# Earlier tiles of a transform, a copy on another engine, and a weight queue served behind the others: one change to a fused spectral and feed-forward kernel on one Trainium2 core

## The chip, the core and the metric

The kernel runs on one core of one Trainium2 chip. A core has five engines, each with its own in-order queue of instructions: TensorE (PE: matrix products into PSUM; PEld is its weight load), VectorE (DVE), ScalarE (ACT), GpSimd (POOL) and SyncE (SP, which here only issues DMAs; ACT and POOL issue some too). Engines wait for each other through semaphores. The metric is the time of one execution on the device in microseconds, lower is better, as the median of several runs.

## What is computed

```python
def _A_ref(x, w_r, w_i):
    X = jnp.fft.rfft2(x, axes=(-2, -1)) * (w_r + 1j * w_i)
    return jnp.fft.irfft2(X, s=(S, D), axes=(-2, -1))

def _B_ref(x, w1, w2):
    h = _silu(jnp.einsum("bsd,df->bsf", x, w1))
    return jnp.einsum("bsf,fd->bsd", h, w2)

xn = _layernorm(x, axis=-1)
return x + _A_ref(xn, w_r, w_i) * _silu(_B_ref(xn, w1, w2))
```

S = 2048 tokens, D = 1024, F = 3584, all float32.

## The kernel before, in words

Matmuls run in float16 on numbers split into a high and a low half, three passes for one product. The 2048 tokens are four chunks c of 512.

**The work that fills TensorE.** The first product (xn by w1, `mm1`, PSUM tile `pa`, 24 matmuls of 512 columns, L466 is the matmul) runs over chunks and feature tiles. The second product (h by w2, `mm2`, PSUM tile `pb`, L549 to L551) is made of seven block products m by eight token tiles j by two halves k of 21 matmuls each; `w2_block` and `SUMMED = (4, 5)` say which blocks of w2 enter product m. Its left operand `ht` is loaded by `load_h` from a queue of ScalarE (L525), two token tiles ahead.

**The background work.** Everything else is written as generators that yield between steps, and their matmuls are slipped between the blocks of the two products. The list `bg` holds the layer norm, the transform over d of each chunk (`fd_gen`), the transform over s (matmuls `fx`), and the inverse of each chunk (`i_gen`, in the order `IORDER = (1, 3, 0, 2)`). The list `wq` holds the splitting of w1 and then of w2 (`w2_gen`), and `xq` the scans for maxima.

**fd_gen.** For a chunk: four tiles p of 24 small matmuls into a PSUM tile `fa` (`fa_mat`, L803 to L805; PSUM tag "ft" with two buffers), two ScalarE instructions that empty it into `L0` (`fa_evac`, L812 and L813; two buffers), a butterfly on VectorE per tile, then four stages j of a radix step on VectorE, whose results ScalarE and VectorE split (`high_r`, L884 and L886; `low_r`) and SP stores.

**w2_gen.** One step loads a tile `jr` of w2 four steps ahead (SP, L420), for m = 4 and 5 lets GpSimd add a second block onto a tile three steps ahead (an accumulating DMA, L424), makes the high half on ScalarE (`high`, L257) and the low half of the tile before on VectorE (`low`, L260).

**i_gen.** `load_i` puts four DMAs of `zt`, one of `kk`, and for the first chunk the constants `cis`, on SP. `edge_in` copies the edge frequencies into `zt` (128 partitions by 16 elements). Then `iu` matmuls (L1281 and L1289; four tiles), with a copy `uc` on ScalarE (L1295) and two VectorE instructions `ub` (L1297, L1298) that free the PSUM tile, further VectorE steps, a split `us`, and a second set of matmuls `id`.

**What sets the order.** `work()` is called once after each block of `mm1` and twice for each (m, j) of `mm2`. It hands out one step of `wq`, one of `xq` in seven calls of eight, and then up to three steps of `bg`, as long as the planner's clock for VectorE is not over that for TensorE by more than `LEAD`; a step's yield says what it costs VectorE. The order in which the steps are handed out is the order of their instructions on every engine's queue.

Of the kernel before, what the change touches and what calls it, by code (L numbers as in the profile page):

```python
# [26 lines left out]
IORDER = (1, 3, 0, 2)  # L27
# [105 lines left out]
def spectral_ffn(ctx, tc, x, w_r, w_i, w1, w2, ca, kc, ci, tw, pm, out):  # L133
    nc = tc.nc
# [35 lines left out]
    zps = cp.tile([128, 2, 4, 4, 2], F16, name="zps")  # L170
# [45 lines left out]
    clock = {"pe": 0.0, "dve": 0.0}  # L216
# [16 lines left out]
    def radix4(sign, b, d, o):  # L233

        sub = nc.vector.tensor_tensor
        plus, minus = ((2, 7), (6, 3)) if sign < 0 else ((6, 3), (2, 7))

        def pick(i):
            st = i[1] - i[0]
            stop = i[1] + (1 if st > 0 else -1)  # L240
            return o[:, i[0]:stop:st]

        sw = d[:, 1, ::-1]
        sub(o[:, 0:2], b[:, 0], b[:, 1], op=OP.add)
        sub(o[:, 4:6], b[:, 0], b[:, 1], op=OP.subtract)
        sub(pick(plus), d[:, 0], sw, op=OP.add)
        sub(pick(minus), d[:, 0], sw, op=OP.subtract)
# [207 lines left out]
    done2, ready2, chunks = [0], [-1], [0]  # L455
# [343 lines left out]
    def fa_mat(c, p):  # L799
        ps = pt.tile([128, 8, 128], F32, name=f"fa{c}_{p}", tag="ft")  # L800
        sl, xt = slice(p * 128, (p + 1) * 128), xnT[c]
        for d in range(8):
            nc.tensor.matmul(ps[:, d], xt[:, 0, d, sl], A["ca"][:, 0, d], start=True, stop=False)  # L803
            nc.tensor.matmul(ps[:, d], xt[:, 0, d, sl], A["ca"][:, 1, d], start=False, stop=False)
            nc.tensor.matmul(ps[:, d], xt[:, 1, d, sl], A["ca"][:, 0, d], start=False, stop=True)  # L805
        psa[c, p] = ps

    def fa_evac(c, p):
        ps = psa.pop((c, p))
        t0 = A["p"].tile([128, 8, 2, 65], F32, name=f"L0_{c}_{p}", tag="L0", bufs=2)  # L810
        nc.gpsimd.memset(t0[:, :, 1, 0:1], 0.0)
        nc.scalar.activation(t0[:, :, 0], ps[:, :, 0:65], AF.Copy)  # L812
        nc.scalar.activation(t0[:, :, 1, 1:64], ps[:, :, 65:128], AF.Copy)  # L813
        l0[c, p] = t0

    def fd_gen(c):
# [51 lines left out]
            tt(v[:, 1, 0:1], ee[:, 0, 0, 0:1], ee[:, 1, 0, 0:1], op=OP.subtract)  # L868

        for i in range(6):  # L870
            if i < 4 and c:
                fa_mat(c, i)
            if 1 <= i <= 4 and (c or i > 2):
                fa_evac(c, i - 1)
            yield 0
            if i >= 2:
                yield from bfly(i - 2)
            yield 0
        o, sp, total, both = {}, {}, {}, {}

        def high_r(j):
            room = ap.tile([128, 2048 + 256 * len(THREE)], F16, name=f"Rs{c}_{j}", tag="Rs", bufs=2)
            both[j] = room[:, 2048:].rearrange("p (q h k) -> p q h k", h=2, k=128)
            nc.scalar.activation(both[j][:, :, 0], total[j], AF.Copy, scale=2.0**-21)  # L884
            sp[j] = room[:, 0:2048].rearrange("p (q h k) -> p q h k", h=2, k=256)
            nc.scalar.activation(sp[j][:, :, 0], o[j], AF.Copy, scale=2.0**-21)  # L886

        def low_r(j):
            nc.vector.scalar_tensor_tensor(sp[j][:, :, 1], o[j], 2.0**-21, sp[j][:, :, 0], op0=OP.mult, op1=OP.subtract)
            nc.vector.scalar_tensor_tensor(both[j][:, :, 1], total[j], 2.0**-21, both[j][:, :, 0], op0=OP.mult, op1=OP.subtract)  # L890
            defer(2, lambda: nc.sync.dma_start(vd[j][:, :, c], sp[j]))
            defer(2, lambda: nc.sync.dma_start(vs[j][:, :, c], both[j]))

        for j in range(4):
            sl = slice(128 * j, 128 * j + 128)
            if j:
                high_r(j - 1)
            b = ap.tile([128, 2, 2, 128], F32, name=f"Rb{c}_{j}", tag="Rb", bufs=1)
            d = ap.tile([128, 2, 2, 128], F32, name=f"Rd{c}_{j}", tag="Rd", bufs=1)
            nc.vector.tensor_tensor(b, vt[:, 0:2, :, sl], vt[:, 2:4, :, sl], op=OP.add)  # L900
            nc.vector.tensor_tensor(d, vt[:, 0:2, :, sl], vt[:, 2:4, :, sl], op=OP.subtract)
            if j:
                low_r(j - 1)
            r = ap.tile([128, 8, 128], F32, name=f"Ro{c}_{j}", tag="Ro", bufs=1)
            radix4(-1, b, d, r)
            o[j] = r.rearrange("a (q r) k -> a q (r k)", r=2)
            total[j] = ap.tile([128, len(THREE), 128], F32, name=f"vt{c}_{j}", tag="E", bufs=1)
            some = o[j][:, THREE[0]:THREE[-1] + 1]
            nc.vector.tensor_tensor(total[j], some[:, :, 0:128], some[:, :, 128:256], op=OP.add)
            clock["dve"] -= 0.8  # L910
            yield 3.9
        high_r(3)
        yield 0.5
# [332 lines left out]
    def edge_in(c):  # L1246
        zt = C["z"][c]
        if c % 2:
            zt = zt.rearrange("m (e q h l i) -> m e q h l i", e=2, q=4, h=2, l=8)
            nc.gpsimd.tensor_copy(zt[:, :, :, :, 0, 0], zps[:, :, c])  # L1250
        else:
            zt = zt.rearrange("m (q h r l i) -> m q h r l i", q=4, h=2, r=2, l=8)
            nc.gpsimd.tensor_copy(zt[:, :, :, :, 0, 0], zp[:, c].rearrange("m r q h -> m q h r"))

    def i_gen(c):
        ip = C["p"]
        tt, stt = nc.vector.tensor_tensor, nc.vector.scalar_tensor_tensor
        if c == IORDER[0]:
            edge_in(c)
# [187 lines left out]
        for p in range(5):  # L1447
            if p < 4:
                mat2(p)
            if p:  # L1450
                bfly(p - 1)
            if p == 3 and c != IORDER[-1]:
                edge_in(IORDER[IORDER.index(c) + 1])
            yield 3.4 if p else 0.3
# [13 lines left out]
    def slot(q):  # L1468
        while q:
            job = q[0]  # L1470
            cost = job.step()
            if not job.done:
                return cost
            if q and q[0] is job:
                q.pop(0)
        return 0
# [19 lines left out]
    with tc.manual_schedule():  # L1496
        bg, wq, xq = [], [], []
# [20 lines left out]
        def after(ev):  # L1518
            settle()
            fresh_ev[0] = ev  # L1520
            tick()
            work()

        def work():
            slot(wq)
            count[0] += 1
            if count[0] % 8:
                slot(xq)
            clock["dve"] = max(clock["dve"], clock["pe"] - 1.0)
            for _ in range(3):  # L1530
                if clock["dve"] > clock["pe"] + LEAD or hold[0] or slot(bg) == PAUSE:
                    break

        nc.gpsimd.memset(ones, 1.0)
        idle = ones.bitcast(F16)
# [34 lines left out]
        for c in range(4):  # L1570
            add(bg, fd_gen(c))
# [69 lines left out]
        for n, (m, j) in enumerate(seq):  # L1641
# [14 lines left out]
            for k in range(2):  # L1656
                while ready2[0] < m * NP + 7 * k + 6:
                    slot(wq)
                mm2(m, j, ps, k)
                if k == 0:  # L1660
                    settle()
                    load_parts(m, j)
                    ahead_rows(m, j)
                    if (m, j) == (6, 6):
                        load_parts(m, 7)
                        ahead_rows(m, 7)
                    tick()
                    work()
# [43 lines left out]
```

## Time and profile before

| | us |
|---|---|
| three runs | 1228.38, 1229.09, 1229.40 |
| median | 1229.09 |
| profiled execution, its own time | 1229.27 |
| its span (first to last instruction) | 1227.5 |
| TensorE busy | 1211.4 |
| VectorE busy | 1003.7 |
| ScalarE busy | 496.1 |
| GpSimd busy | 140.2 |

All times in the views are microseconds from the start of the span. A row of the timeline gives start, duration, engine, line, operation, out<-in, partitions by elements, the count, and in brackets how long the engine had stood idle before it and what released it. In the chain of waits a row gives start, duration and what the chain passed through. Names in the profile are without the buffer numbers that the order of instructions shows.

### The profile page before, as it was taken

To read this page: it belongs to the slowest core of one execution; us is meant where nothing else is said; L and a number is where in the kernel's file an instruction comes from. 1 tells how busy PE (TensorE), PEld (TensorE's weight loads), DVE (VectorE), ACT (ScalarE), POOL (GpSimd) and SP (SyncE) were. 2 spreads that over 40 slices of the span, in tenths; PEclk is the share of its full clock that TensorE was granted. 3 is DMA by queue.
4 is the path that set the end of the run, shared out by engine and by line. 5 is a ranking of instruction groups with operands and counts; after the bars stand their busy time and mean duration, and the time that the engine had idled before them with its cause. 6 is when DMAs were issued, how large, how long until landed. Compare 5 with 4: busy or idle time off the path is not lost.

```text
span 1227.5 us, 19143 instructions
## 1 busy us (share of the span) xinstructions
PE 1211.4 (99%) x6992; PEld 615.1 (50%) x6992; DVE 1003.7 (82%) x2006; ACT 496.1 (40%) x670; POOL 140.2 (11%) x256
## 2 busy tenths in 40 slices
PE   8999999999999999999999999999999999999998
PEld 5544445445444544445445555554445554455545
DVE  7778997898798798958969989995377876997766
ACT  6775553455375654434423222221122322333212
POOL 3320100002010000201101121152111111000000
PEclk9999999999999999999999999999999999999999
DMA  8887585747678978489998999977979999996677
GB/s 251 184 195 188 165 255 180 211 130 214 192 254 276 317 231 270 146 259 208 188 282 279 263 253 233 315 255 221 269 218 302 264 338 310 305 364 244 224 249 274
DMA packets 285055, 299.98 MB, mean 244 GB/s; under 512 B 48928, under 2 KB 211744, under 8 KB 284576
## 3 DMA queue, kind: packets, MB, share of 16 engines
q1 hardware_dynamic: 264944, 239.95, 66.9%
q10 hardware_dynamic: 15840, 50.67, 11.8%
q0 software_dynamic: 4176, 8.13, 3.6%
q8 instruction: 55, 0.90, 0.3%
q14 instruction: 40, 0.33, 0.1%
HBM read 188.05 MB, written 104.35 MB: 238 GB/s over the span
## 4 chain that ended last, share of the span: by engine, by line
PE 59%; DMA 15%; DVE 14%; ACT 3%; issue 3%; SPq 1%; POOL 1%; ACTq 0%; DVEq 0%; POOLq 0%
PE pa L466 33%; PE pb L551 7%; PE pb L549 7%; PE pb L550 7%; DMA jr<-in_B_w_dram 2%; PE id L1371 2%; DMA jr<-ws 1%; DVE Z L1124 1%; DVE w L260 1%; DMA cis<-in_ci_dram 1%; DMA ht<-hd_dif 1%; ACT xp L750 1%; DMA vq<-vd 1%; DMA zd<-zq 1%; DMA zt<-zd 1%
## 5 line engine op out<-in xcount | busy, mean ns | idle before, releaser
L466 PE MATMUL pa<-xnT,w 128*128 128x512 f16 x2688 | 584.3, 379 | 1.3 <-ACT w L257 0.7
L466 PEld LDWEIGHTS <-w 128*128 128x128 f16 x2688 | 261.2, 98 | 312.7 <-issue 1.2
L549 PE MATMUL pb<-w,ht 128*128 128x512 f16 (+2 forms) x812 | 300.4, 372 | 0.0
L550 PE MATMUL pb<-w,ht 128*128 128x512 f16 (+2 forms) x812 | 300.4, 372 | 0.0
L551 PE MATMUL pb<-w,ht 128*128 128x512 f16 (+2 forms) x812 | 300.3, 372 | 0.0
L551 PEld LDWEIGHTS <-ht 128*128 128x128 f16 x812 | 79.4, 98 | 91.1
L549 PEld LDWEIGHTS <-ht 128*128 128x128 f16 x812 | 79.5, 98 | 86.7
L550 PEld LDWEIGHTS <-ht 128*128 128x128 f16 x812 | 79.4, 98 | 86.8
L475 ACT ACTIVATE h<-pa,s 128x512 f32<-128x512 f32 x112 | 75.6, 677 | 77.6 <-PE pa L466 60.2
L257 ACT ACTIVATE w<-jr,sc 128x512 f16<-128x512 f32 x98 | 68.4, 713 | 86.4 <-DMA jr<-in_B_w_dram 45.6
L260 DVE SCALAR_TENSOR_TENSOR w<-jr,sc,w 128x512 f16<-128x512 f32 x98 | 71.3, 743 | 18.8 <-ACT w L257 18.8
L257 ACT ACTIVATE hosum<-hr,hs 128x1536 f16<-128x1536 f32 x28 | 44.0, 1573 | 87.5 <-DVE hr L505 34.9
L260 DVE SCALAR_TENSOR_TENSOR hoone<-h,hs,hoone 128x2048 f16<-128x2048 f32 x28 | 65.6, 2342 | 7.2 <-ACT hoone L257 7.2
L257 ACT ACTIVATE hoone<-h,hs 128x2048 f16<-128x2048 f32 x28 | 55.9, 1995 | 28.6 <-issue 11.1
L504 DVE TENSOR_TENSOR hr<-h 128x1024 f32<-128x1024 f32 x28 | 34.1, 1219 | 21.8 <-ACT h L475 21.8
L260 DVE SCALAR_TENSOR_TENSOR hosum<-hr,hs,hosum 128x1536 f16<-128x1536 f32 x28 | 50.7, 1810 | 1.4 <-ACT hosum L257 1.4
L257 ACT ACTIVATE w<-w1r,rs 128x1024 f16<-128x1024 f32 x28 | 31.9, 1143 | 37.7 <-DVE w L260 24.2
L642 ACT ACTIVATE pl<-pl,c 128x512 f32<-128x512 f32 (+2 forms) x28 | 17.7, 656 | 70.2 <-DVE pl L618 43.6
L424 POOL DMA_DIRECT2D jr<-in_B_w_dram x28 | 24.6, 999 | 180.3 <-DMA jr<-in_B_w_dram 89.7
L1124 POOL TENSOR_TENSOR Z<-yb 128x32 f32<-128x32 f32 x32 | 16.2, 525 | 209.0 <-DVE yb L1103 202.2
L1033 ACT ACTIVATE zq<-Z,zs 128x1024 f16<-128x1024 f32 x16 | 18.4, 1148 | 52.5 <-DVE Z L1124 25.6
L260 DVE SCALAR_TENSOR_TENSOR w<-w1r,rs,w 128x1024 f16<-128x1024 f32 x28 | 35.6, 1273 | 2.3 <-ACT w L257 2.2
(239 smaller groups left out, 1571.6 us busy)
## 6 DMA issues: line engine op xcount, KB each, us to landing
w1r<-in_B_w_dram SPq DMA_DIRECT2D x28, 512.0 KB, 6.6
hd_sum<-hosum SPq DMA_DIRECT2D x56, 256.0 KB, 2.9
hd_one<-hoone SPq DMA_DIRECT2D x56, 256.0 KB, 4.0
hd_dif<-hoone SPq DMA_DIRECT2D x56, 256.0 KB, 4.3
w2m<-in_B_w_dram SPq DMA_DIRECT2D x28, 512.0 KB, 5.6
ht<-hd_dif ACTq DMA_DIRECT2D x32, 448.0 KB, 9.2
jr<-in_B_w_dram SPq DMA_DIRECT2D x56, 256.0 KB, 6.7
ht<-hd_sum ACTq DMA_DIRECT2D x32, 448.0 KB, 5.7
```

What stands on the lines that cost most here:

```text
L257: nc.scalar.activation(hi, raw, AF.Copy, scale=scale)
L260: nc.vector.scalar_tensor_tensor(lo, raw, scale, hi, op0=OP.mult, op1=OP.subtract)
L424: nc.gpsimd.dma_start(raw[n], w2_block(*todo[n], 1), accum_op=OP.add)
L466: nc.tensor.matmul(ps, w[:, wh, d], xt[:, xh, d], start=(n == 0), stop=(n == 23))
L475: nc.scalar.activation(hq[:, 2 * (c % 2) + f % 2], ps, AF.Silu, scale=s1[:, f:f + 1])
L504: tt(sums[:, 0:2], hq[:, 0::2], hq[:, 1::2], op=OP.subtract)
L549: nc.tensor.matmul(ps, hh[:, 0], w[:, 0], start=first, stop=False)
L550: nc.tensor.matmul(ps, hh[:, 0], w[:, 1], start=False, stop=False)
L551: nc.tensor.matmul(ps, hh[:, 1], w[:, 0], start=False, stop=last)
L1033: nc.scalar.activation(zqs[q][:, 0, :, 16 * j:16 * j + 16], zs_[u], AF.Copy, scale=zs)
L1124: eng.tensor_tensor(Z[:, ns, pos], x0[:, :, ls], x1[:, :, ls], op=o_)
L1371: nc.tensor.matmul(ps[:, g, cols], us[g][:, uh, 4 * r + p], C["ci"][:, ch, g, r, cols], start=(r == 0 and n == 0), stop=(r == 1 and n == 2 ...
```

## The change

Five edits. (1) In `fd_gen` the chunks after the first no longer issue one tile per step: tile 2's matmuls come at step 0 and tile 3's at step 3, and the emptying of tiles 1, 2, 3 at steps 0, 3 and 4. (2) Tiles 0 and 1 of the next chunk are issued in stages j = 2 and 3 of the chunk before, with the emptying of tile 0 at j = 3. (3) The planner's clock for VectorE gets 0.5 back per stage in place of 0.8. (4) `edge_in` for the first inverse chunk (c = 1) copies on VectorE in place of GpSimd. (5) In the second product (`chunks[0] == 4`) the step of `wq` is handed out behind those of `bg` in a call of `work()`, in place of ahead of them.

```diff
@@ fd_gen
         for i in range(6):
-            if i < 4 and c:
-                fa_mat(c, i)
-            if 1 <= i <= 4 and (c or i > 2):
-                fa_evac(c, i - 1)
+            if i in (0, 3) and c:
+                fa_mat(c, 2 + i // 3)
+            if i in (0, 3, 4) and (c or i):
+                fa_evac(c, max(i, 2) - 1)
             yield 0
...
         for j in range(4):
+            if j > 1 and c < 3:
+                fa_mat(c + 1, j - 2)
+                if j > 2:
+                    fa_evac(c + 1, 0)
             sl = slice(128 * j, 128 * j + 128)
...
-            clock["dve"] -= 0.8
+            clock["dve"] -= 0.5
             yield 3.9
@@ edge_in
-            nc.gpsimd.tensor_copy(zt[:, :, :, :, 0, 0], zps[:, :, c])
+            (nc.vector if c == IORDER[0] else nc.gpsimd).tensor_copy(zt[:, :, :, :, 0, 0], zps[:, :, c])
@@ work
-            slot(wq)
+            if chunks[0] < 4:
+                slot(wq)
             count[0] += 1
             if count[0] % 8:
                 slot(xq)
...
+            if chunks[0] == 4:
+                slot(wq)
```

Three places show how instructions move. The first is ScalarE around chunk 3's transform over d (`fa_p` is the PSUM tile of tile p, `L_3_p` what it is emptied into, `h` the evacuation of the first product's `pa`, `w` and `junk` work on the weights). Before:

```order
L257 ACTIVATE w_21_4185<-w1r_3823,rs_228 128x1024
L390 ACTIVATE junk,w2m<-w2m_3977 128x1024
L812 ACTIVATE L_3_0_4219<-fa_0_4126 128x8x65
L813 ACTIVATE L_3_0_4219<-fa_0_4126 128x8x63
L475 ACTIVATE h_8_1_4109<-pa_16_4151,s_229 128x512
L390 ACTIVATE junk,w2m<-w2m_4016 128x1024
L812 ACTIVATE L_3_1_4292<-fa_1_4194 128x8x65
L813 ACTIVATE L_3_1_4292<-fa_1_4194 128x8x63
```

Of the change:

```order
L812 ACTIVATE L_3_0_4032<-fa_0_3927 128x8x65
L813 ACTIVATE L_3_0_4032<-fa_0_3927 128x8x63
L884 ACTIVATE Rs_2_4036<-vt_2_3966 128x2x128
L886 ACTIVATE Rs_2_4036<-Ro_2_3961 128x4x256
L475 ACTIVATE h_8_0_3916<-pa_16_3968,s_229 128x512
L390 ACTIVATE junk,w2m<-w2m_3883 128x1024
L884 ACTIVATE Rs_3_4093<-vt_3_4050 128x2x128
L886 ACTIVATE Rs_3_4093<-Ro_3_4045 128x4x256
L475 ACTIVATE h_8_0_3916<-pa_17_4052,s_229 128x512
L812 ACTIVATE L_3_1_4168<-fa_1_4007 128x8x65
L813 ACTIVATE L_3_1_4168<-fa_1_4007 128x8x63
```

Tile 0 of chunk 3 is now emptied ahead of the last two splits (`Rs`) of chunk 2, and tile 1 three evacuations of `pa` after it. On TensorE two blocks of `pa` lie between `fa_0` and `fa_2` of that chunk before, and now three beside `fa_1`.

The second place is VectorE and ScalarE at the first inverse chunk (`w_3_1` is half of w2's tiles for m = 3, `jr` a loaded tile of it, `kept` an evacuation of `pb`, `ub` the inverse's first VectorE step). VectorE before, where the copy of zt's edge stood on GpSimd behind the joins of jr_8644, jr_8675 and jr_8701 as `L1250 COPY zt_8581<-zps 128x16`:

```order
L260 SCALAR_TENSOR_TENSOR w_3_1_8544<-jr_8504,sc_234,w_3_1_8544 128x512
L260 SCALAR_TENSOR_TENSOR w_3_1_8544<-jr_8542,sc_234,w_3_1_8544 128x512
L598 TENSOR_TENSOR kept_7103<-kept_7103,pb_5_8652 128x512
L260 SCALAR_TENSOR_TENSOR w_3_1_8544<-jr_8572,sc_234,w_3_1_8544 128x512
L260 SCALAR_TENSOR_TENSOR w_3_1_8544<-jr_8619,sc_234,w_3_1_8544 128x512
L598 TENSOR_TENSOR kept_7180<-kept_7180,pb_6_8710 128x512
L1297 TENSOR_TENSOR ub_0_8840<-iu_0_8788,uc_0_8838 128x512
```

VectorE with the change:

```order
L260 SCALAR_TENSOR_TENSOR w_3_1_8544<-jr_8542,sc_234,w_3_1_8544 128x512
L598 TENSOR_TENSOR kept_7103<-kept_7103,pb_5_8652 128x512
L260 SCALAR_TENSOR_TENSOR w_3_1_8544<-jr_8588,sc_234,w_3_1_8544 128x512
L1254 COPY zt_8577<-zps 128x16
L260 SCALAR_TENSOR_TENSOR w_3_1_8544<-jr_8619,sc_234,w_3_1_8544 128x512
L598 TENSOR_TENSOR kept_7180<-kept_7180,pb_6_8710 128x512
L1301 TENSOR_TENSOR ub_0_8840<-iu_0_8788,uc_0_8838 128x512
```

On SP the load of jr_8572 stood ahead of the four zt loads, kk and cis; that of jr_8588, which takes its place in the sequence of w2's tiles, now stands behind them, next to jr_8619. On ScalarE the two issues of ht_0 stand, before and now, between the high half of that tile (jr_8572, now jr_8588) and that of jr_8619.

The third place is ScalarE at the third inverse chunk (`w_5_1`: w2's tiles for m = 5; `pl` a sum of partial products). Before:

```order
L525 DMA ht_7_1_10428<-hd_one_1_97 128x1792
L257 ACTIVATE w_5_1_10302<-jr_10299,sc_234 128x512
L1295 ACTIVATE uc_0_10520<-iu_0_10470 128x512
L1341 ACTIVATE up_0_10526<-ub_0_10522 128x8
L1342 ACTIVATE up_0_10526<-ub_0_10522 128x8
L642 ACTIVATE pl_4_1_10383<-pl_4_1_10383,c_233 128x512
```

Of the change:

```order
L525 DMA ht_7_1_10428<-hd_one_1_97 128x1792
L1299 ACTIVATE uc_0_10516<-iu_0_10466 128x512
L1345 ACTIVATE up_0_10522<-ub_0_10518 128x8
L1346 ACTIVATE up_0_10522<-ub_0_10518 128x8
L257 ACTIVATE w_5_1_10302<-jr_10299,sc_234 128x512
L642 ACTIVATE pl_4_1_10383<-pl_4_1_10383,c_233 128x512
```

The high half of jr_10299 moved from ahead of the inverse's three instructions to behind them.

## The prediction

> **What bounds the kernel now.** I read the page first: share of busy time, granted clock, DMA.
>
> ```profile
> span 1227.5 us, 19143 instructions
> PE 1211.4 (99%) x6992; PEld 615.1 (50%) x6992; DVE 1003.7 (82%) x2006; ACT 496.1 (40%) x670; POOL 140.2 (11%) x256
> PEclk9999999999999999999999999999999999999999
> ```
>
> TensorE is busy 99% of the span at full granted clock. The changed program holds the same matmuls as the old one, only some in another place. So time can leave only where TensorE stands still, and the next view is what it waited for (engine, line, what it waited for: us in total, times, longest).
>
> ```profile
> PE tp L759 <- ACT x L750: 2.7, 2, 2.5
> PE iu L1281 <- POOL zt L1250: 2.6, 1, 2.6
> PE iu L1289 <- DVE ub L1298: 1.8, 1, 1.8
> PE fa L803 <- ACT L L813: 1.3, 1, 1.3
> ```
>
> The row for tp belongs to the start, which the change leaves alone. The other three are single events, one wait each. The timeline places them and gives their full size (start, duration; a matmul's 0.38 overlaps its successor, which starts 0.22 later).
>
> ```profile
> 410.27 2.97 PE L466 MATMUL pa<-xnT,w 128*128 128x512 f16 x13
> 414.58 0.22 PE L803 MATMUL fa<-cas,xnT 128*128 128x128 f16 x1 [1.34 <-ACT L L813]
> 876.51 0.38 PE L550 MATMUL pb<-w,ht 128*128 128x512 f16 x1
> 876.73 0.38 PE L551 MATMUL pb<-w,ht 128*128 128x512 f16 x1
> 879.72 2.85 PE L1281 MATMUL iu<-kk,zt 128*128 128x128 f16 x48 [2.61 <-POOL zt L1250]
> 1036.64 0.38 PE L551 MATMUL pb<-w,ht 128*128 128x512 f16 x1
> 1038.83 1.55 PE L1289 MATMUL iu<-kk,zt 128*128 128x129 f16 x24 [1.81 <-DVE ub L1298]
> ```
>
> Start to start, less the 0.22 that a matmul takes anyway (876.73 − 876.51): 879.72 − 876.73 − 0.22 = 2.77 us lost at the first inverse chunk's iu_0; 1038.83 − 1036.64 − 0.22 = 1.97 at the third inverse chunk's iu_2; and, since the thirteen pa matmuls end at 413.24 and the last of them began 0.38 earlier, at 412.86, 414.58 − 412.86 − 0.22 = 1.50 at chunk 3's fa_2. Together 6.24 us, 0.51% of the span. That is the most that these edits can win.
>
> **First edit: the transform's first tiles sooner (the fd_gen loops and the planner's 0.5).** The chain of waits before 414.58 runs on ScalarE:
>
> ```profile
> 413.95 0.59 ACT L L813
> 414.58 0.22 PE fa L803
> 401.32 0.22 PE L805 MATMUL fa<-cas,xnT 128*128 128x128 f16 x1
> ```
>
> fa_2 needs the PSUM buffer of fa_0, whose last matmul starts at 401.32; ScalarE, in its order, empties it only by 413.95 + 0.59 = 414.54, 13.2 us later. Before, two products of 24 matmuls lie between fa_0 and fa_2, 2 × 24 × 0.216 = 10.4 us (0.216 is the 0.22 unrounded: thirteen starts from 410.27 to 412.86 are twelve steps). After the change, three lie there (15.6 us), beside fa_1, so a ScalarE exactly as late as now is 2.4 us early. The evacuations themselves are the same two instructions per tile, moved and not added. fa_3 behind fa_1 has at least five products of cover. The work that is brought forward, two tiles of 24 small matmuls, costs nothing: it is issued while VectorE runs the previous chunk's radix stages. Without that cover it would cost its own wait on ScalarE, 1.34, as now. Term: −1.50; bounds −1.50 and 0.
>
> **Second edit: the copy of zt's edge from GpSimd to VectorE, first inverse chunk only.** The chain of waits up to 879.72, and the engines' timelines beside it:
>
> ```profile
> 849.21 11.20 DMA zt<-zd
> 860.43 14.25 DMA cis<-in_ci_dram
> 874.75 2.60 DMA jr<-in_B_w_dram
> 877.35 0.61 POOL jr L424 x2
> 878.41 1.27 POOL zt L1250
> 876.66 2.74 POOL L424 DMA_DIRECT2D jr<-in_B_w_dram  x3 [41.31 <-DMA jr<-in_B_w_dram]
> 875.37 0.72 ACT L257 ACTIVATE w<-jr,sc 128x512 f16<-128x512 f32 x1 [21.93 <-DMA jr<-in_B_w_dram]
> 876.12 0.75 DVE L260 SCALAR_TENSOR_TENSOR w<-jr,sc,w 128x512 f16<-128x512 f32 x1 [11.22 <-ACT w L257]
> 401.78 0.15 DVE L299 TENSOR_TENSOR ep<-e 128x1 f32<-128x1 f32 x1
> ```
>
> zt itself does not make iu_0 late: GpSimd takes its queue in order, and three joins (L424, accumulating loads of w2) stand ahead of the copy, waiting for jr loads that the SP queue put behind zt and cis. On VectorE the three joins are no longer ahead. But something else is, as the order shows: the low half L260 of jr_8588, whose load the third edit has just moved behind zt, kk and cis on the SP queue. Its place there is the one that jr_8619 has before, whose high half starts at 875.37. So the new path is high 0.72, low 0.75, then the copy: 875.37 + 0.75 + 0.75 = 876.87 (the old rows' own starts, 876.12 then 0.75), and the copy's 16 elements a lane. No row shows that copy on VectorE: 0.15 by the nearest small VectorE row, 1.27 by GpSimd's own. I take 0.15, since it is VectorE that runs it: zt complete at 877.0, with 878.1 as the other end. TensorE is there at 876.95, or at 875.45 if the 1.50 of the first edit arrives in full. So iu_0 waits between nothing and 877.05 − 875.45 = 1.6 us, against 2.77 + 1.50 that could be won up to here. Two things shorten that: loads issued from planner steps move up with TensorE, and the two ht_0 loads of the next product, which now run inside the same stretch, leave it (next edit). I take 0.5 as the rest: term −2.77 + 0.5 = −2.27; bounds −2.77 and −0.1 (copy 1.27, no transfer earlier).
>
> [...]
>
> **Third edit: w2's step behind those of transform and inverse in the second product.** It changes no count, only who stands first on ScalarE, VectorE, GpSimd and the SP queue when one call of the planner issues several. The gain is in the chain to 1038.83:
>
> ```profile
> 1036.25 0.72 ACT L257 ACTIVATE w<-jr,sc 128x512 f16<-128x512 f32 x1 [11.88 <-DMA jr<-in_B_w_dram]
> 1036.87 0.59 ACT uc L1295
> 1037.48 0.69 DVE L1297 TENSOR_TENSOR ub<-iu,uc 128x512 f32<-128x512 f32 x1 [7.99 <-ACT uc L1295]
> 1038.18 0.61 DVE ub L1298
> ```
>
> ScalarE stands 11.88 us at the high half of jr_10299, until its accumulating join has landed, and only behind it comes the copy uc that iu_2 waits for through ub. In the new order uc stands ahead of that high half and the inverse step on VectorE ahead of the low half. ScalarE was free for 11.88 us, so uc runs as soon as iu_0 is done: iu_2 does not wait. Term −1.97; bounds −1.97 and 0 (the next high half takes the place). VectorE stood still for 7.99 us before ub; the ub step now falls in there, which also eases the us chain behind it.
>
> What it costs: high halves of 0.72 now stand ahead of some ht issues on ScalarE's queue. In the second product's m = 1 that is one more ahead of ht_2:
>
> ```profile
> 729.88 3.18 ACTq L525 DMA_DIRECT2D ht<-hd_dif  x2
> DMA to landing us min/median/max: 9.4/10.8/13.8
> 742.41 0.38 PE L549 MATMUL pb<-w,ht 128*128 128x512 f16 x1
> ```
>
> Issued at 729.88, landed 9.4 later at the earliest, 739.3; pb_2 starts at 742.41 without a wait, so its margin is 0 to 3.1, and the delay 0.7 to 1.4: a cost of 0 to 1.4, where I take 0.2. The one large move is at the first inverse chunk: ht_0's two issues stand behind the high half of jr_8588, so they go from 854.48 to about 875.4.
>
> ```profile
> 854.48 4.86 ACTq L525 DMA_DIRECT2D ht<-hd_sum  x2
> 875.45 0.81 ACTq L525 DMA_DIRECT2D ht<-hd_sum  x2
> 882.41 0.38 PE L549 MATMUL pb<-w,ht 128*128 128x512 f16 x1
> ht<-hd_sum ACTq DMA_DIRECT2D x32, 448.0 KB, 5.7
> ```
>
> They are used by the next product's pb_0, which follows the half block of 21 matmuls at 882.41 (21 × 0.216 = 4.5) and iu_2 (1.3): 888.3 before, about 884.5 with the gains (1.50 + 2.27 earlier). Issue 875.45 + 5.7 (the median of this form) = 881.2, with 13.8 from the slowest ht seen 889.3: cost 0 to 4.9, taken as 0.1.
>
> Sum: −1.50 − 2.27 − 1.97 + 0.2 + 0.1 = −5.44. Against the profiled execution's own 1229.27 (1.8 outside its span) that is 1223.83; the median of the runs is 0.18 lower, so 1223.65, rounded 1223.7.
>
> **The rivals.** What a measurement here can tell from no change is about 0.2%, 2.46 us: faster is below 1226.6, slower above 1231.6.
>
> A. *The copy stays late.* VectorE's copy ends at 878 or after (a slow copy, a hold by GpSimd, or jr_8588 landing later than jr_8619 did) and TensorE still starts iu_0 near 879.7. Then the first edit's gain is lost in the same wait too, since TensorE merely arrives earlier, and only the third term and what lies behind 880 is won: −1.97 + 0.3, 1227.4; with a copy ending at 878.1 it is −1.6 more, 1225.8. For it: the copy's place directly behind a w2 low half. Against: the 2.6 us between 877.05 and 879.67.
>
> B. *Transfers take the gain back.* The DMA shares are high where the gains fall (columns: window, sum, five engines, clock, DMA share, GB/s):
>
> ```profile
> 880.00:960.00 80.00, 80.00 (x546) 43.77 (x543) 58.18 (x154) 22.29 (x41) 13.28 (x17) 1.00 0.96 260
> 960.00:1040.00 80.00, 78.19 (x517) 42.06 (x516) 62.33 (x151) 22.26 (x42) 7.69 (x11) 1.00 0.96 304
> 1040.00:1140.00 100.00, 100.00 (x626) 52.42 (x624) 89.35 (x190) 34.33 (x64) 1.13 (x2) 1.00 0.85 297
> ```
>
> If loads cannot move up with TensorE, later ht or w2 tiles become the wait: half of 5.44 gone is 1226.4, all but the third term 1227.1. Against: TensorE does not wait once for an ht or a w2 tile in the second product now, through 260 us of such shares.
>
> C. *Slower: ht_0 starves pb_0.* One mechanism: w2's step behind the inverse's puts jr_8588's load behind zt, kk and cis, its high half waits for it on ScalarE (21.93 now for jr_8619), and ht_0 queues behind that. If ht_0 comes with ht_1 and the three joins in one burst, it may land far after 884.5. From 884.5 + 5.4 = 889.9 on (14.5 us after issue) nothing is left of the gain; from 892.4 on, 17 after issue, the kernel is slower. A landing at 896 gives 1235. Longest seen: 13.8, so a small chance.
>
> D. *The transform's edit does not do what it says.* ScalarE's lateness grows by as much as the tiles move, and fa_2 waits as now: 1.50 back, 1225.2. It counts as faster still.
>
> **How the numbers follow.** Forecast as summed, 1222.4 to 1225, 0.62; D 0.06; A 0.13, of which a third ends below 1226.6; B 0.12, half of it below; C 0.07 (0.06 slower, 0.01 within). Faster: 0.62 + 0.06 + 0.05 + 0.06 = 0.79. Same: 0.08 + 0.06 + 0.01 = 0.15. Slower 0.06. The low end is all three stalls gone with no cost, 1229.09 − 6.24 = 1222.85, less 1.0 for what an easier VectorE may give elsewhere and the spread of the runs: 1221.8. The high end takes in A and B to 1228.3. The likeliest case's own range is 1222.4 to 1225.0.
>
> **What would show it.** In the new profile's list of TensorE's waits the row fa <- ACT L should be gone; the row iu <- POOL zt replaced by none or by iu <- DVE zt of under 1.6; the row iu <- DVE ub gone. TensorE's busy time should stay near 1211 and the span fall to about 1222. New rows pb <- DMA ht near 742, 805 or 885 would show the third edit's cost. A row iu <- DVE zt above 2 means A; pb <- DMA ht of more than 5 means C; many small rows pb <- DMA mean B. The prediction fails if the order of issue moves a transfer that I have taken as fixed.

## The result, and the profile after

The change is slower. Ten runs of each kernel, side by side: 1234.61 us (1229.64 to 1238.35) against 1229.59 us (1225.93 to 1232.63) before, ratio 1.0039 with a 95% interval of 1.0025 to 1.0053. The profiled execution took 1233.81 us. Its page:

```profile
span 1232.0 us, 19135 instructions
PE 1216.2 (99%) x6992; PEld 617.0 (50%) x6992; DVE 1003.4 (81%) x2007; ACT 494.4 (40%) x670; POOL 126.8 (10%) x255
PEclk9999999999999899999999999999999999999999
```

The span grew by 4.5 us and TensorE's busy time by 4.8, with the same matmuls. One slice of the granted clock shows an 8. What TensorE waited for:

```profile
PE pa L466 <- ACT h L475: 4.5, 2, 4.3
PE eps L1165 <- POOL edge L1158: 2.0, 1, 2.0
PE tp L759 <- ACT x L750: 1.8, 3, 1.2
```

All three waits that the change was to remove are gone: no row for fa, none for iu. Two others stand in their place, one in the first product and one at the edge matmuls (`eps`) of the transform over s. TensorE and VectorE at the first and third inverse chunk:

```profile
886.23 2.84 PE L1285 MATMUL iu<-kk,zt 128*128 128x128 f16 x48
1036.07 2.91 PE L1293 MATMUL iu<-kk,zt 128*128 128x129 f16 x48
1043.35 1.54 PE L1293 MATMUL iu<-kk,zt 128*128 128x129 f16 x24
881.86 0.75 DVE L260 SCALAR_TENSOR_TENSOR w<-jr,sc,w 128x512 f16<-128x512 f32 x1 [8.34 <-ACT w L257]
882.53 0.20 DVE L1254 COPY zt<-zps 128x16 f16<-128x16 f16 x1
```

The copy ran behind the low half of w2, as the order said, took 0.20 us, and was done 3.5 us before iu_0. The iu rows carry no brackets: nothing was waited for. For iu_0 that is partly luck: TensorE came to it at 886.23, where it came at 876.95 before, because the two new waits had held it up. In the run with three repairs (below), where they are gone, iu_0 does wait, 0.71 us start to start.

The first new wait, on TensorE, ScalarE and the SP queue (SPq rows are the DMAs that SP issues):

```profile
398.47 5.34 PE L466 MATMUL pa<-xnT,w 128*128 128x512 f16 x24
408.07 12.21 PE L466 MATMUL pa<-xnT,w 128*128 128x512 f16 x45 [4.26 <-ACT h L475]
406.08 0.42 ACT L884 ACTIVATE Rs<-vt 128x256 f16<-128x256 f32 x1 [8.74 <-DMA vs<-Rs]
407.35 0.67 ACT L475 ACTIVATE h<-pa,s 128x512 f32<-128x512 f32 x1
396.12 1.20 SPq L498 DMA_DIRECT2D hd_sum<-hosum  x2
398.88 0.91 SPq L891 DMA_DIRECT2D vd<-Rs  x1
399.85 1.04 SPq L892 DMA_DIRECT2D vs<-Rs  x1
```

ScalarE stood 8.74 us before the split `Rs` of stage 3. There are two Rs buffers, so stage 3 takes over that of stage 1, whose stores SP issued only at 398.88 and 399.85; the second landed at 406. The planner defers these stores by two ticks (a tick comes with each call of the planner), and on SP's queue they stood behind the stores of `hosum` (L498, a part of h), for which SP had waited 5.9 us. The same splits of stages 1 and 3 before, with the store between them:

```profile
384.45 0.40 ACT L884 ACTIVATE Rs<-vt 128x256 f16<-128x256 f32 x1
394.43 0.71 SPq L892 DMA_DIRECT2D vs<-Rs  x1
405.41 0.40 ACT L884 ACTIVATE Rs<-vt 128x256 f16<-128x256 f32 x1
```

There the split of stage 3 came 11 us after the store was issued and waited for nothing. In the change, behind the split in ScalarE's queue stood the evacuation of pa (L475, 407.35), without which TensorE had no PSUM buffer. The last matmul before began at 398.47 + 5.34 − 0.38 = 403.43, so 408.07 − 403.43 − 0.22 = 4.42 us were lost.

The granted clock behind it, and behind the second new wait (window, sum, busy time of five engines, clock, DMA share, GB/s):

```profile
408.00:410.00 2.00, 1.93 (x5) 0.71 (x5) 2.00 (x3) 1.00 (x3) 0.00 (x0) 0.50 1.03 174
412.00:414.00 2.00, 2.00 (x9) 0.80 (x8) 1.86 (x5) 2.00 (x4) 0.85 (x2) 0.79 1.08 391
414.00:416.00 2.00, 2.00 (x11) 0.87 (x9) 1.97 (x6) 2.00 (x3) 0.00 (x0) 1.00 1.06 344
816.00:820.00 4.00, 4.00 (x13) 1.55 (x12) 4.00 (x8) 0.00 (x0) 0.00 (x0) 0.62 1.03 403
```

After the stall TensorE ran at half its clock until 412.84, 4.8 us from its start at 408.07: its matmuls start 0.43 us apart there, 5 of them in the 2 us from 408, where 11 do at full clock from 414, 0.22 apart. Adding up how much later than 0.216 us each start came gives 2.37 us behind the first stall and 1.71 behind eps, whose wait is here:

```profile
812.21 0.40 PE L1165 MATMUL eps<-edge,perm 128*128 128x24 f32 x2 [2.01 <-POOL edge L1158]
811.79 0.37 POOL L1158 COPY edge<-xsv 128x24 f32<-128x24 f32 x1
810.00 1.02 POOL L1128 TENSOR_TENSOR Z<-yb 128x32 f32<-128x32 f32 x2 [16.77 <-DVE yb L1107]
```

GpSimd's edge copies stand behind its share of the Z step and came 2.18 us late (start to start). The balance: −6.24 for the three stalls, +4.42 + 2.37 at 408, +2.18 + 1.71 at eps: +4.44, against a span 4.5 longer. What remains is small: TensorE was 0.4 us ahead by 130 us, and eps' 18 matmuls took 0.2 us longer (2.34 against 2.11).

### The profile page after: what moved, and what is told of

Its sections match the earlier page's. It is cut to its first block, busy times and chain, and to the rows that moved or that the text cites. A ratio compares the mean times of both kernels' runs of the same rounds, so it can differ in the third digit from the quotient of the medians.

```text
span 1232.0 us, 19135 instructions
## 1 busy us (share of the span) xinstructions
PE 1216.2 (99%) x6992; PEld 617.0 (50%) x6992; DVE 1003.4 (81%) x2007; ACT 494.4 (40%) x670; POOL 126.8 (10%) x255
## 4 chain that ended last, share of the span: by engine, by line
PE 71%; DMA 9%; DVE 9%; ACT 3%; issue 2%; SPq 1%; ACTq 0%; POOL 0%; DVEq 0%
PE pa L466 33%; PE pb L551 11%; PE pb L549 11%; PE pb L550 11%; PE id L1375 2%; DMA jr<-ws 2%; DMA ws<-wd 2%; DMA ht<-hd_dif 1%; ACT xp L750 1%; DMA wq<-in_A_w_r_dram 1%; PE iu L1293 1%; PE iu L1285 1%; DMA wq<-in_A_w_i_dram 1%; DMA ht<-hd_sum_d 1%; DVE Z L1128 1%
## 5 line engine op out<-in xcount | busy, mean ns | idle before, releaser
L475 ACT ACTIVATE h<-pa,s 128x512 f32<-128x512 f32 x112 | 75.2, 676 | 62.8 <-PE pa L466 47.7
```

Source lines behind the costliest of these rows:

```text
L475: nc.scalar.activation(hq[:, 2 * (c % 2) + f % 2], ps, AF.Silu, scale=s1[:, f:f + 1])
```

## The experiments

Unless said otherwise, each was timed side by side with the kernel before; the ratio is to it. Theory S: the splits of the transform over d now stand too near each other for their buffer's store.

**Which edit loses.** Four kernels: edits 1 to 3 alone, edit 5 alone, edit 4 alone, edits 4 and 5. They differ from the kernel before only by those lines of the diff above.

> Edits 1 to 3 alone (transform over d, planner's 0.5). Theory S (the split of stage 3 now stands two blocks of pa behind that of stage 1, whose buffer it reuses, and waits on ScalarE for that buffer's store; TensorE then starves for an evacuation and its clock falls): the stall of 4.4 us near 408 is here again with the same granted clock of 0.5 behind it, the wait on fa (1.5) is gone, so 4.4 + 2.2 - 1.5 = 5.1 us slower than before, ratio 1.003 to 1.006. Rival W (the w2 queue behind the others is what loses): 1.5 us faster, ratio 0.9988.

> Edit 5 alone (w2's step behind those of transform and inverse in the second product). Theory S: the wait of iu on ub (1.97) goes, the wait of iu on GpSimd's copy stays about as it is (2.8), so 1 to 2 us faster if the edge matmuls (eps), which had 0.3 us to spare before, are in time; if they are late by 2 us with a clock drop, up to 3 us slower. Rival W: 4 us slower or more, with eps waiting on GpSimd and the granted clock down behind it, and nothing wrong near 408.

> Edit 4 alone (the first inverse chunk's edge copy on VectorE). Both theories: the wait of iu on GpSimd's copy (2.77) goes, since with w2's step ahead as before no load of w2 behind cis stands ahead of the copy on VectorE but that of jr_8572, which is early; 2 to 2.8 us faster, ratio 0.9978 to 0.9984; 0 if the copy is held until GpSimd's joins are through.

> Edits 4 and 5 without the transform's. Theory S: both waits of iu gone, 4 to 4.7 us faster (ratio 0.9962 to 0.9968), less up to 3 if eps is late here too; granted clock 1.0 throughout the first product. Rival W: not faster, since the loss comes with edit 5.

| edits | median us | ratio | 95% interval |
|---|---|---|---|
| 1 to 3 | 1236.55 | 1.0050 | 1.0034 to 1.0067 |
| 5 | 1228.39 | 0.9987 | 0.9972 to 1.0001 |
| 4 | 1227.52 | 0.9979 | 0.9966 to 0.9992 |
| 4 and 5 | 1228.01 | 0.9987 | 0.9973 to 1.0002 |

TensorE's waits with edits 1 to 3 alone:

```profile
PE pa L466 <- ACT h L475: 5.8, 2, 4.2
PE iu L1285 <- POOL zt L1254: 1.8, 1, 1.8
PE iu L1293 <- DVE ub L1302: 1.6, 1, 1.6
PE s L266 <- ACT h L475: 1.1, 1, 1.1
```

The loss is in edits 1 to 3, as expected: the stall near 408 is back, with another near 532 (1.29 + 1.80 us start to start), and the two waits of iu are still there because nothing was done about them. Rival W falls. Edit 4 alone, too, gave what was expected of it (0.9978 to 0.9984).

Edit 5 alone left neither wait of iu in its profile, though the one on GpSimd had been expected to stay. It went by a narrow margin: the three joins still stand ahead of the copy on GpSimd, but the first is issued at 873.93 in place of 876.66, the copy ends at 876.93, and iu_0 starts at 876.99. The same order makes iu_0 wait 1.67 us for that copy in the run with early edge copies (below). So edits 4 and 5 overlap in part; that together they gained no more than each, within these intervals, has a second reason in eps, which in the profile of both was late by 0.88 and then lost 1.5 us of clock. The expectation of 4 to 4.7 us for both holds only with its clause on eps. With edit 4 alone, the copy and GpSimd's joins ran at the same time:

```profile
877.18 4.51 POOL L424 DMA_DIRECT2D jr<-in_B_w_dram  x5 [41.09 <-DMA jr<-in_B_w_dram]
877.33 0.20 DVE L1250 COPY zt<-zps 128x16 f16<-128x16 f16 x1
```

0.20 us, as in the changed kernel: the hold by GpSimd that rival A and the expectation name did not show.

**Does the store make the stall?** The stores of the splits one planner tick sooner, all else as in the change.

```diff
-            defer(2, lambda: nc.sync.dma_start(vd[j][:, :, c], sp[j]))
-            defer(2, lambda: nc.sync.dma_start(vs[j][:, :, c], both[j]))
+            defer(1, lambda: nc.sync.dma_start(vd[j][:, :, c], sp[j]))
+            defer(1, lambda: nc.sync.dma_start(vs[j][:, :, c], both[j]))
```

> The whole change, but the stores of the transform's splits are handed out one planner tick sooner (defer 1 in place of 2), so that the buffer that the split of stage 3 takes over is free one block (5.2 us) sooner; the order on TensorE, ScalarE and VectorE stays. Theory S: the wait of ScalarE on the store (8.7 us) shrinks to 3.5 or less, TensorE no longer waits near 408 and keeps its clock, 6 to 7 us faster than the change (ratio to before 0.996 to 0.999, the edge matmuls' 2 us deciding which). Rival T (the evacuations of fa or the longer ScalarE work crowd out the evacuation of pa whatever the store does): as slow as the change, ratio 1.003 or more.

Measured 1231.91 us, 1.0018 (0.9999 to 1.0037). Its waits:

```profile
PE pa L466 <- ACT h L475: 1.7, 1, 1.7
PE eps L1165 <- POOL edge L1158: 1.4, 1, 1.4
PE s L266 <- ACT h L475: 0.3, 1, 0.3
```

The stall near 408 is gone. The store of stage 1 and the split of stage 3:

```profile
390.69 0.59 SPq L892 DMA_DIRECT2D vs<-Rs  x1
398.98 0.42 ACT L884 ACTIVATE Rs<-vt 128x256 f16<-128x256 f32 x1 [2.90 <-DVE vt L913]
```

The store now goes out ahead of hosum's, 9 us sooner and not only the 5.2 of one block, and the split waits for VectorE's result and no longer for the store. The 1.7 in the list is another wait, at 526. So the store was the cause of the stall at 408, and rival T falls by the profile. By time the run decides nothing: 1.0018 lies between the two expectations, and its interval overlaps that of the change. Some 2.7 us were won, not 6 to 7; eps still lost 1.52 us and 2.3 of clock in this profile.

**The same with the copy left on GpSimd** (edits 1, 2, 3, 5 and early stores).

> Edits 1, 2, 3 and 5 with the stores one tick sooner, the edge copy left on GpSimd. Theory S: as the run with all edits and early stores within 1 us, since w2's step behind the others already puts the joins behind the copy on GpSimd: ratio 0.996 to 0.999 and no wait of iu on GpSimd over 1 us. If the copy on VectorE matters by itself: iu waits on GpSimd's copy by 1.5 us or more and this run is that much slower than the run with all edits and early stores.

1233.51 us, 1.0025 (1.0008 to 1.0042): slower than expected, with no wait of iu. The intervals of the two overlap, so a gain of the copy on VectorE beside edit 5 cannot be told here. Nor could this run show it: TensorE, held up earlier, came to iu_0 at 883.15, 1.55 us after GpSimd's copy had ended.

**A larger planner credit** (`clock["dve"] -= 0.8` in the change, as before). On ScalarE three blocks of pa then lie between the splits of stages 1 and 3.

> The whole change with the planner's credit of 0.8 as before in place of 0.5. On ScalarE three blocks of pa then lie between the splits of stages 1 and 3 of chunk 2, against two in the change and four before. Theory S: the store has one block more, the wait at that split is 3 to 4 us in place of 8.7 and TensorE's stall near 408 gone or under 1, so 4 us or more faster than the change (ratio to before 0.996 to 1.000). Rival T: no better than the change, 1.003 or more, since the same instructions are on ScalarE.

A miss in time: 1235.81 us, 1.0054 (1.0036 to 1.0071). At the split of chunk 2's stage 3 (395.84) ScalarE does not wait for the store, and the stall near 408 is gone; a wait of 5.4 us on a store at 284.88, in another chunk, costs TensorE nothing. But a different stall cost as much as the old one:

```profile
383.60 1.06 ACT L283 ACTIVATE junk<-w1r 128x1024 fp8e4<-128x1024 f32 x1 [14.05 <-DMA w1r<-in_B_w_dram]
391.22 0.22 PE L803 MATMUL fa<-cas,xnT 128*128 128x128 f16 x1 [4.17 <-ACT L L813]
```

Here ScalarE stands 14.05 us before a scan of a w1 tile that has not landed, and the evacuation of fa (390.10 to 391.17) stands behind it. That wait also moves the two splits 28 us apart (367.63 and 395.84), so the run is no clean test of S against T. What it shows is that tiles of fa issued earlier can wait on whatever ScalarE happens to be held by.

**What a stall costs beside its length.** The kernel before with 16 stalls of chosen length added to the first product: four small matmuls, k copies of their PSUM tile on ScalarE, and a tiny matmul that waits for them. The added work leaves the output as it is.

```diff
+        GATES = {30 + 4 * k: k % 8 + 1 for k in range(16)}
...
+            for _ in range(GATES[n]):
+                nc.scalar.activation(ps, ps, AF.Copy)
+            nc.scalar.activation(gh, ps[:, 0:16], AF.Copy, scale=0.0)
...
+            nc.tensor.matmul(pb[0:16, 0:16], gh, gh, start=True, stop=True)
```

> The kernel before with 16 added stalls of TensorE in the first product: four small matmuls, a chain of 1 to 8 ScalarE copies of their PSUM tile, and a tiny matmul that waits for the chain (added work; the output is the same). It measures what a stall costs beside itself. Theory G (the granted clock falls only where TensorE was idle for about 4 us): gaps under 2 us are followed by matmuls at 0.216 us a start, gaps over 4 us by some at 0.43, at a cost of 1 to 2.5 us each, with chance between. Rival: the slow matmuls near 408 have to do with the place (ScalarE or DMA at that time) and not with the gap: then most of the long gaps here are followed by full clock.

One execution was run, the profiled one (1312.65 us). Four of the waits:

```profile
239.51 0.18 PE L1594 MATMUL gateb<-gate 128*16 128x16 f16 x1 [2.17 <-ACT gate L1592]
263.49 0.18 PE L1594 MATMUL gateb<-gate 128*16 128x16 f16 x1 [2.73 <-ACT gate L1592]
458.71 0.18 PE L1594 MATMUL gateb<-gate 128*16 128x16 f16 x1 [2.11 <-ACT gate L1592]
487.01 0.18 PE L1594 MATMUL gateb<-gate 128*16 128x16 f16 x1 [2.73 <-ACT gate L1592]
```

The first two kept the granted clock, the other two lost it. By the loss from start to start, five of the 16 stalls kept the clock (1.05, 1.05, 1.67, 2.34 and 2.89 us); two of 2.28 and 2.89 lost it; and all nine of 3.5 to 7.4 lost it, for 1.28 to 2.87 us each in late starts. It does not hang on the place in the kernel, so the rival falls; theory G is right on the stalls under 2 us and over 4, but its "about 4 us" is too long.

What sets equal stalls apart shows in the trace's record of the granted clock. In each of the 14 profiles of this document all changes of the clock lie on one grid of 3.413 us, whose place differs from run to run (three falls here begin at 288.93, 486.90 and 889.68, 58 and 118 steps apart; the change's two before its end begin at 406.02 and 815.62, 120 steps apart, and last until 412.84 and 819.03), and here every fall but the one at the end of the run lasts one, two or three of its steps. The steps around the two waits of 2.73 us (TensorE's busy time is the second number behind the window, the clock the third from the end):

```profile
258.21:261.62 3.41, 2.55 (x15) 1.19 (x13) 3.41 (x7) 0.79 (x2) 0.00 (x0) 1.00 0.00 0
261.62:265.04 3.42, 1.55 (x8) 0.78 (x9) 1.12 (x2) 3.33 (x5) 0.00 (x0) 1.00 0.78 235
483.49:486.90 3.41, 0.79 (x7) 0.38 (x5) 1.67 (x12) 2.46 (x5) 0.00 (x0) 1.00 1.08 249
486.90:490.31 3.41, 3.30 (x9) 1.27 (x10) 1.34 (x1) 3.41 (x4) 0.00 (x0) 0.50 0.72 266
```

The first wait falls across the end of a step: TensorE idles 0.86 us in one and 1.87 in the next, and the clock stays. The second lies almost whole in one step, which idles 2.62, and the next step runs at half clock. Over the 14 profiles, past 105 us, the clock fell after every step at full clock with 2.03 us or more of idle TensorE, and after none with 1.87 or less (of two between, 1.97 fell and 2.00 did not), but for steps in which eps' 18 tiny matmuls follow their wait: there 0.8 to 1.5 us were enough, and once, in the change, the fall came a step later (2.01 us idle in the step from 808.79, the fall at 815.62). In the kernel before, no step in that stretch idled more than 1.81 us and none was followed by a fall; in the change the step from 402.61 idled 2.21, and the clock fell at its end.

**The edge copies.** Edit 5 alone, with GpSimd's edge copies handed out ahead of its share of the Z step of u = 13.

```diff
             tt(d2, Y[:, 0:2], Y[:, 2:4], op=OP.subtract)
-            if u > 13:
+            if u > 12:
                 next(B["edge"])
...
-            if u > 12:
+            if u > 13:
                 next(B["edge"], None)
```

> Edit 5, with GpSimd's copies for the edge matmuls handed out one step earlier, ahead of its share of the Z step of u = 13 in place of behind it. Theory E (with edit 5 these copies come too late for eps in most runs, and eps' 18 tiny matmuls behind a wait of a microsecond make the clock fall, so that 2 to 4 us go back): no wait of eps on GpSimd, no slow matmuls near 805, median 2 to 3 us under that of edit 5 alone (1228.4), ratio 0.9955 to 0.9975. Rival: eps is late only by chance, and this is as edit 5 alone, 0.9987.

A miss in time: 1228.98 us, 0.9989 (0.9975 to 1.0003), as edit 5 alone, which is what the rival said; in the profile of edit 5 alone eps had not been late either. Here, too, eps waits for nothing, but fa (1.65 us) and iu_0 (1.67 us, on GpSimd's copy) do. The granted clock, which the profiled execution kept at 1.000, was 0.996 to 0.999 in 9 of the 12 runs. What lowered it in those is open, since only one execution is profiled.

**Both repairs in the whole change** (early stores, early edge copies).

> The whole change with both repairs: stores of the splits one tick sooner, and GpSimd's edge copies one step earlier. Theory S with E: what is left of the loss is the wait near 525 (2.2 us and 1.7 of clock), so 3 to 4 us faster than with early stores alone (1231.9): ratio 0.998 to 1.000. If something else in the change is slow, it stays at 1.0015 or more.

1230.55 us, 0.9997 (0.9984 to 1.0010), within the expected ratio, though by medians 1.4 us under early stores alone and not 3 to 4: the loss is gone, the gain is not there. What is left is a stall near 527 (2.43 + 1.80 us start to start) with the fall of the clock behind it, and 0.96 us at iu_0. The rows that lead to this stall stand so in the change itself, where VectorE's order is new too:

```profile
519.94 1.22 DVE L285 TENSOR_REDUCE m1b<-w1r 128x1 bf16<-128x1024 f32 x1 [4.86 <-DMA w1r<-in_B_w_dram]
521.08 0.68 DVE L904 TENSOR_TENSOR Rb<-V 128x512 f32<-128x512 f32 x1
525.55 1.22 DVE L509 TENSOR_TENSOR h<-h 128x1024 f32<-128x1024 f32 x1
526.85 2.00 ACT L257 ACTIVATE hoone<-h,hs 128x2048 f16<-128x2048 f32 x1 [10.79 <-DVE h L509]
```

VectorE waits for a tile of w1, and then the whole last radix stage of chunk 3 (L904 on) runs ahead of L509, for which ScalarE waits with evacuations of pa behind it. In the kernel before L509 stood ahead of that stage. In the change's own profile it came almost in time: TensorE waited 0.20 us for the evacuation, at 531.

**Other tiles of the transform moved.** Edits 4, 5, both repairs, and instead of edits 1 to 3 only tiles 2 and 3 one step later.

```diff
-            if i < 4 and c:
-                fa_mat(c, i)
-            if 1 <= i <= 4 and (c or i > 2):
-                fa_evac(c, i - 1)
+            if i in (0, 1, 3, 4) and c:
+                fa_mat(c, i - i // 3)
+            if i in (1, 2, 4, 5) and (c or i > 3):
+                fa_evac(c, i - 1 - i // 4)
```

> Edits 4 and 5, both repairs, and in place of edits 1 to 3 only tiles 2 and 3 of the transform one step later (matmuls at steps 0, 1, 3, 4, evacuations at 1, 2, 4, 5), no tile in the chunk before. Theory S with E: none of the three old stalls and none of the new ones, granted clock 1.0 but at the start; 6 us faster than before, ratio 0.994 to 0.996. If the moved tiles again place the split of stage 3 too near that of stage 1 (three blocks here), a wait on L475 near 400 is back: 1.000 or more.

1227.66 us, 0.9980 (0.9969 to 0.9992): faster than before, but by 2 us where 6 were expected. fa waits no more, and a wait of pa on L475 of 2.7 us near 397 has come for it; iu_0 waits 1.49. The store has no part in that wait of pa: ScalarE had stood 14.65 us before the scan of a w1 tile, until 384.06, and then worked without a pause, so that it came late to the evacuation. Here it is the crowding of ScalarE that costs, the thing that rival T had named.

**The third repair.** The whole change, both repairs, and the last radix stages of chunk 3 held back so that L509 stands ahead of them again (against the change; the two repairs are not shown again).

```diff
-            clock["dve"] -= 0.5
+            clock["dve"] -= 0.5 if c < 3 or j < 2 else -1.0
```

> The whole change with three repairs: stores of the splits one tick sooner, GpSimd's edge copies one step earlier, and the last radix stages of chunk 3 held back by the planner (credit of -1.0 at its stages 2 and 3), so that VectorE makes h (L509) ahead of the radix stage of chunk 3 as before the change. Theory S in full (the change loses only through these three new waits and the clock behind them): no stall left between 105 us and the end but under 1.5, granted clock near 1.0; 4 to 6 us faster than before, ratio 0.995 to 0.9975. Rival (a replaced wait always finds another place, or the change costs something that no wait shows): 0.998 or more.

1223.32 us (1222.15 to 1225.56; before 1230.54), 0.9947 (0.9931 to 0.9963). The profiled span is 1221.5 us, 6.0 shorter than before. L509 stands at 516.93, ahead of L904 at 519.19, and the stall near 527 is gone. TensorE's waits of 0.5 us or more, and the first inverse chunk:

```profile
PE tp L759 <- ACT x L750: 2.9, 3, 2.3
PE spin L1549 <- POOL ones L1541: 1.0, 1, 1.0
PE pa L466 <- ACT w L257: 0.7, 1, 0.7
PE iu L1285 <- DMA jr<-in_B_w_dram: 0.6, 1, 0.6
PE pa L466 <- DMA xnT<-xs: 0.5, 1, 0.5
```

```profile
875.31 0.20 DVE L1254 COPY zt<-zps 128x16 f16<-128x16 f16 x1
875.72 2.84 PE L1285 MATMUL iu<-kk,zt 128*128 128x128 f16 x48 [0.55 <-DMA jr<-in_B_w_dram]
```

Past 105 us only the wait of iu_0 is left, 0.71 us start to start. The profile names a load of w2 for it, but iu_0 starts 0.21 us after the copy on VectorE has ended, as in the two other profiles in which it waits with the copy there (0.96 and 1.49 us, above), so the copy is the likelier cause. Theory S in full holds, with a little more than the 4 to 6 us expected; the rival falls, and this kernel is faster than both the kernel before and the change.

## Why the prediction was wrong

**What bounds the kernel, and the three terms.** Right, with some luck in one of them. All three stalls went in the change: 6.24 us where 5.74 net of iu's rest were counted. That iu_0 did not wait at all came of TensorE's being 9.3 us late there; with the three repairs it waits 0.71, for the 0.5 taken as the rest and within the bounds of 0 and 1.6. The copy cost 0.20 us for the 0.15 taken. A hold of that copy by GpSimd, one of rival A's three grounds, is shown by no run: with edit 4 alone the copy took 0.20 us, too, while GpSimd's joins ran. Rivals A, B, C and D did not come in the change: no wait of TensorE on ht, none on w2, none on fa. (One bound is off by 0.1: 889.3 less 884.5 is 4.8.)

**The step that failed** is in the first edit: "The work that is brought forward, two tiles of 24 small matmuls, costs nothing: it is issued while VectorE runs the previous chunk's radix stages." The cover was named, but what the edit does to the covering work was not looked at. Edits 1 to 3 also move the radix stages. In ScalarE's order four evacuations of pa lie between the splits of stages 1 and 3 of chunk 2 before, and two in the change; the rows of the first place above show Rs_2 and Rs_3 a single pa apart. They were read for fa alone (and the emptying of tile 1 comes two evacuations of pa after that of tile 0 in them, not three). A split takes over a buffer that a deferred store must have left. With two blocks (10.4 us) less between the splits ScalarE waited 8.74 us for that store, and TensorE lost 4.42 for the evacuation behind it and 2.37 in the clock after that, where the prediction had nothing. Early stores removed exactly this wait, which shows it. Which of edits 1 to 3 moves the stages, and that the planner does so because fa's matmuls count on its clock for TensorE, was not tried by itself; the second is read from the code.

**The price of a stall** was also mis-sized. Each was counted as its own length, since the granted clock was 1.0 in the profile of before. A stall of 3.5 us or more cost 1.3 to 2.9 on top, in all nine that were added. Shorter ones lost the clock as well: waits of 2.1 and 2.7 us that lay in one step of the grid, the second almost whole, were enough, and so were eps' waits of 0.7 to 2.3 with 18 tiny matmuls behind them, all five times. So a stall that the change moves or makes is dear once it is long, and for that it was to be read.

**eps.** The margin of the edge matmuls was not looked up: it was 0.3 us before (GpSimd's first copy ended at 804.55, eps began at 804.84). With edit 5 they were late by 0.9 to 2.5 us (start to start) in five of the six profiled kernels that left GpSimd's copies where they were, and in none of the four with the copies a step earlier. That edit 5 is what makes them late is not shown: they were late by 0.85 in the run with added stalls too, which has no edit 5, and with edit 5 alone they had 0.8 to spare.

**The range** ended at 1228.3. Rivals A to C lay in the second product, and D, in the first, gave back only the 1.50 of fa; none took an evacuation of pa as its place. Of the 10.9 us between 1223.7 and 1234.61, 6.8 are, by the one profile, the stall at 408 with its clock and 3.9 eps with its clock.

## What to carry to other kernels

When a table or planner hands work out sooner, read the new order of every engine for the neighbours of what was moved, and ask of each instruction that came forward what frees its buffer and when that store was issued; a wait in front of a queue is paid by whatever stands behind it (here ScalarE's 8.74 us at a split, of which 4.42 reached TensorE through the evacuation behind it). Before counting a removed stall as won, look for the next waits with margins under a microsecond, and price any new one with the clock that can fall behind it (here 1.3 to 2.9 us more for each added stall of 3.5 us or longer). A change that shifts everything is best judged after repairing the two or three accidents that it makes: here the same edits with three repairs went from 1.0039 to 0.9947.

## What was not expected of the hardware

The spread of the runs goes with the granted clock. In 90 runs of the kernel before that stood beside these experiments (1225.6 to 1234.8 us), the 14 with a granted clock of 1.000 have a median of 1227.33, and the 11 at 0.996 or below one of 1232.05. That the place of the stalls on the grid of 3.413 us makes this spread is the author's estimate and was not shown, since no second execution of that kernel was profiled. In the one that was, the stall of 2.77 us at iu_0 fell across the end of a step (1.32 and 1.29 us idle) and kept the clock, and the stall of 1.97 left 1.81 in one step. Shifted against the grid by a microsecond or two, the longer one would have lain in one step, as the added wait of 2.73 us did behind which the next step ran at half clock. A single profile with a clock of 1.0, as the one that the prediction was read from, hides that.
